# Left keys of two neighbouring head groups in one pass of 64x32 tiles

## The chip, the cores and the metric

The kernel runs on one core of one Trainium2 chip. The metric is the device time of one execution in microseconds (us), given as the median of several runs. A core has TensorE (PE in the profile, with its weight loads as PEld), VectorE (DVE), ScalarE (ACT), GpSimd (POOL) and SyncE (SP); each follows its own instruction list, and semaphores hold them together. Matmuls write into PSUM, which has eight banks, each 128 partitions by 512 float32.

## The reference

Inputs are q, k and v of 8 batches, 12 heads, 448 positions and 64 dimensions. Queries and keys are normalized by their root mean square, then comes softmax attention, and the result goes through a feed-forward network that has no nonlinearity but a product:

```
q_n, k_n = rmsnorm(q, g_q), rmsnorm(k, g_k)
scores = q_n @ k_n.T / sqrt(64)
attn = softmax(scores)            # over the 448 keys
x = (attn @ v) as [3584 tokens, 768]
out = ((x @ w1) * (x @ w2)) @ w3 @ w_out     # d_ff = 1024
```

## The kernel before

**Tiling.** The 96 heads are taken as 24 head groups `i` of HQ = 4 heads; three groups make a batch. All matmuls work on parts of the 128x128 array, several at a time: a pass is one set of matmuls that fill the array together and stream 448 (or 384) columns once. Scores come out transposed, with keys on the partitions. A head has 448 keys, that is three blocks of 128 and 64 left over. The left keys of two heads share one 128-partition tile `Pr`: partitions 0 to 63 hold those of one head and 64 to 127 those of the other.

**Scores** (`do_score`, L602): seven units a group, each of four matmuls of 64x64 tiles in one pass (L623), into two neighbouring banks, row half `u` into bank `u`. ScalarE takes the exponential of both banks in one instruction (L645) into the tile `P`, or `Pr` for the seventh unit. There are three `P` buffers; the third lies in the space of `w_outs` and is used once the product w3·w_out is made.

**Values** (`do_pv_kind`, L667): for each group three kinds: 0 is the sums of the exponentials (weights of ones), 1 and 2 are the two halves of the 64 value dimensions. A kind is J = 4 passes of four 128x32 tiles, one column tile a head, all into one bank (L677). The first three passes take the full blocks of keys, the fourth takes `Pr`. As `Pr` holds two heads, the value tile's fourth block is zero in the half that belongs to the other head (memset at L1149), and for the sums `ones[:, 1]` and `ones[:, 2]` are zero in one half. After kind 0 ScalarE makes the reciprocal as Ln and Exp (L692, L693); after kinds 1 and 2 VectorE multiplies it into `xT` (L712).

**FFN** (`Pair`, `do_pass`, L753 to L786): once three groups have filled a batch's `xT`, its FFN becomes a stock of pairs in `waiting`. A pair uses two neighbouring banks in two phases; in each phase a row half writes one of the banks, and at the hand-over (L741) they swap, after a wait through another engine's queue. At most two pairs are open. Names in the profile: `xT,w1s` and `xT,w2s` are the first layer, `w34s,abT` the second; `w34s` is w3·w_out.

**Order.** All instruction orders are written by a planner that runs when the kernel is built: it simulates the engines with fixed durations and at each moment lets `pe_try` (L1070) choose TensorE's next work. It goes on with a block of values that is begun (`pv_state`); else with a running pair; else with transposes, a score (if two neighbouring banks are idle and fewer than two scores are out), a pair that is past its hand-over, values (`pv_ready`, with two idle banks), or a new pair. `pv_ready` (L655) asks that all seven exponentials of the group are done and its values landed. It then starts a group alone if TensorE already is in that mode, if w3·w_out is not finished, or if fewer than `LOW` pairs are in stock; otherwise it also waits for the next group, so that two groups follow each other. `load_v` (L352) brings a group's values in four transfers on POOL's queue, planned when the buffer of four groups earlier is free.

Of the kernel before, what the change touches and what calls it, by code (L numbers as in the profile page):

```python
# [19 lines left out]
INF = float("inf")  # L20
SEM = 0.05
# [174 lines left out]
def kernel(  # L196
# [13 lines left out]
    nc = tc.nc  # L210
# [33 lines left out]
    MAX_PAIRS = 2  # L244
    MARGIN = 0.25
    LOW = 2
    AHEAD_W3 = 4
    EARLY = 4
    STOCK = 14
# [102 lines left out]
    def load_v(i, z):  # L352


        b, m = divmod(i, NQB)
        g, hi = divmod(z, 2)
        p0 = HP * (g ^ hi)
        j0, j1 = (J, NJ) if hi else (0, J)
        src = v[b, HQ * m : HQ * (m + 1)].rearrange("h (p j) d -> p h j d", j=NJ)
        nc.gpsimd.dma_start(  # L360
            out=v_bufs[i % 4][p0 : p0 + HP, g::2, 0 : j1 - j0].rearrange(
                "p h j d -> p h (j d)"
            ),
            in_=src[:, g::2, j0:j1].rearrange("p h j d -> p h (j d)"),
        )
# [236 lines left out]
    def do_score(t, z):  # L602
        n = next_score[0]
        next_score[0] += 1
        last_score[0] = t
        i, g = divmod(n, NU)
        s = st[i]
        if g == 0:
            x = min(range(3), key=lambda x: (p_free(x) > t, x))
            s["P"] = p_bufs[x]  # L610
            p_used[x] = i
            s["Pr"] = p_pool.tile([NP, 2, S], BF, tag="Pr", name="Pr")
        took = pass_us(S) + into("n")
        qkT, sc = s["qkT"], ps_all[:, z : z + 2]
        for c in range(2):
            if g < 2 * NF:
                pr, blk = divmod(g, NF)
                j = blk if c == pr else J + blk
            else:
                pr, j = c, NF  # L620
            cols = slice(HP * pr, HP * pr + HP)
            for u in range(2):
                nc.tensor.matmul(  # L623
                    out=sc[HP * c : HP * c + HP, u, 0:S].rearrange(
                        "p (j s) -> p j s", j=NJ
                    ),
                    lhsT=qkT[u * D : (u + 1) * D, 1, j, cols],
                    rhs=qkT[u * D : (u + 1) * D, 0, :, cols],
                    start=True, stop=True, tile_position=(u * D, HP * c),
                )  # L630
        dst = (
            s["P"][:, pr::2, blk, :] if g < 2 * NF else s["Pr"]
        )
        bank_at[z] = bank_at[z + 1] = INF
        out_scores[0] += 1

        def done(e):
            bank_at[z] = bank_at[z + 1] = e + SEM
            out_scores[0] -= 1
            p_at[i].append(e + SEM)  # L640

        at = t + took + TO_ENGINE - pass_us(S) + 0.187
        add(
            "ACT", 0.80, QUAD * i + 1.8 * g,
            lambda: nc.scalar.activation(out=dst, in_=sc[:, :, 0:S], func=AF.Exp),  # L645
            needs=[lambda: at - 0.187], done=done,
        )
        if g == NU - 1:
            qkT_used[i] = t + took + 0.2
        return took  # L650
# [1 line left out]
    next_pv = [0]  # L652
    pv_state = []

    def pv_ready(t):  # L655
        i = next_pv[0]
        if i >= NQ or all_of(p_at[i], NU) > t or landed[i]["v"] + SEM > t:
            return False
        b, m = divmod(i, NQB)
        if m == 0 and b >= 3 and x_used[b - 3] > t:  # L660
            return False
        stock = sum(p.name != "w" for p in waiting)
        if mode[0] == "v" or all_of(w34_at, CF) > t or i + 1 >= NQ or stock < LOW:
            return True
        return all_of(p_at[i + 1], NU) <= t and landed[i + 1]["v"] + SEM <= t

    def do_pv_kind(t, i, kind, z):  # L667
        s = st[i]
        b, m = divmod(i, NQB)
        ps = ps_all[:, z, 0:S]  # L670
        for j in range(J):
            for hd in range(HQ):
                if kind:
                    w = v_bufs[i % 4][:, hd, j, kind - 1 :: 2]
                else:
                    w = ones[:, 0 if j < NF else 1 + hd % 2, :]
                nc.tensor.matmul(  # L677
                    out=ps[hd * HALF : (hd + 1) * HALF, :],
                    lhsT=w,
                    rhs=s["P"][:, hd, j, :] if j < NF else s["Pr"][:, hd // 2, :],  # L680
                    start=(j == 0), stop=(j == J - 1),
                    tile_position=(0, hd * HALF),
                )
        took = J * pass_us(S) + into("v")
        at = t + took + TO_ENGINE_WIDE - pass_us(S)
        bank_at[z] = INF
        if kind == 0:
            s["r_at"] = INF

            def reciprocal():  # L690
                s["r"] = att_pool.tile([128, S], FP, tag="r", name="r")
                nc.scalar.activation(out=s["r"], in_=ps, func=AF.Ln)  # L692
                nc.scalar.activation(out=s["r"], in_=s["r"], func=AF.Exp, scale=-1.0)  # L693

            def done(e):
                bank_at[z] = e - 0.48 + SEM
                s["r_at"] = e + SEM

            add("ACT", 1.06, -1000.0, reciprocal, needs=[lambda: at], done=done)
            return took  # L700
        if b not in xT:
            xT[b] = x_pool.tile([128, CM, S], BF, tag="xT", name="xT")

        def mul_done(e):
            bank_at[z] = e + SEM
            x_at[b].append(e + SEM)
            if len(x_at[b]) == CM:
                push_ffn(b)

        add(  # L710
            "DVE", 0.53, -1000.0,
            lambda: nc.vector.tensor_tensor(  # L712
                out=xT[b][:, 2 * m + kind - 1, :], in0=ps, in1=s["r"], op=MULT
            ),
            needs=[lambda: at, lambda: s["r_at"]], done=mul_done,
        )
        if kind == 2:
            pv_end[i] = t + took + 0.2
            v_free[i % 4] = t + took + 0.2
            if i + 4 < NQ:  # L720
                plan_load_v(i + 4, -1.0)
        return took

# [339 lines left out]
    def pe_step(t):  # L1065

        took = pe_try(t, t - MARGIN)
        return pe_try(t, t) if took is None else took

    def pe_try(t, r):  # L1070
        idle = idle_banks(r)
        if pv_state:
            i, kind = pv_state[0]
            z = single(idle)
            if z is None:
                return None
            took = do_pv_kind(t, i, kind, z)
            pv_state.clear()
            if kind == 2:
                next_pv[0] += 1  # L1080
            else:
                pv_state.append((i, kind + 1))
            return took
        if mode[0] == "v" and len(idle) >= 1 and pv_ready(r):
            i = next_pv[0]
            took = do_pv_kind(t, i, 0, single(idle))
            pv_state.append((i, 1))
            return took
        two = adjacent(idle)
        score = score_ready(r) and out_scores[0] < 2 and two is not None  # L1090
        hungry = free["ACT"] <= t + 0.3 and out_scores[0] == 0
        if mode[0] == "t":
            took = any_turn(t, r, idle, 1)
            if took is not None:
                return took
        if running[0] and running[0].ready() <= r:
            if score and hungry:
                return do_score(t, two)
            return do_pass(running[0], t)
        took = any_turn(t, r, idle, 2)  # L1100
        if took is not None:
            return took
        new = next_pair(r)
        late = [p for p in pairs if p.ready() <= r]
        if score:
            left = [z for z in idle if z not in (two, two + 1)]
            if hungry or late or new is None or adjacent(left) is not None:
                return do_score(t, two)
        if late:
            return do_pass(late[0], t)  # L1110
        want_pv = pv_ready(r)
        if want_pv and len(idle) >= 2:
            i = next_pv[0]
            took = do_pv_kind(t, i, 0, single(idle))
            pv_state.append((i, 1))
            return took
        if two is not None and new is not None and not want_pv:
            waiting.remove(new)
            start_pair(new, two)
            return do_pass(new, t)  # L1120
        if next_pv[0] == NQ and not waiting and not pairs and last_x[0] < 2 and idle:
            if tile_at(B // 2 - 1, NT - 1) + SEM <= r:
                return do_last(t, single(idle))
        return any_turn(t, r, idle, 1)
# [125 lines left out]
```

## Time and profile before

| what | value |
|---|---|
| median of 7 runs | 363.49 us (361.83 to 364.42) |
| profiled execution | 363.53 us, span 361.8 us |
| granted TensorE clock | 0.997 |
| PE busy | 348.9 us (96%), 7326 matmuls |
| ACT busy | 263.0 us (73%) |
| DVE busy | 207.3 us (57%) |
| matmuls of values and sums on full blocks | 864 (480 + 240 + 96 + 48) |
| matmuls of left keys (`Pr`) | 288 (192 + 96) |
| exponentials (L645) | 168, 915 to 921 ns each |

The span is the time from the first to the last instruction on the core; the execution's own time is measured around it and is 1.7 us longer. A matmul of 448 columns is listed with about 0.35 us, but the next pass starts 0.19 us after it, since matmuls overlap in the array: passes are priced by the distance of their starts. The busy time of PE counts the overlapped time once.

### The profile page before, as it was taken

Reading aid. Unit: us, or ns where it says so; the run is one execution under the profiler, and the core shown is the slowest. Engines: PE = TensorE matmul, PEld = TensorE weight load, DVE = VectorE, ACT = ScalarE, POOL = GpSimd, SP = SyncE. Lnnn points to the kernel's source line nnn. Section 1 sums busy time; section 2 is a strip of 40 time slices with the busy share of each in tenths; the row PEclk is TensorE's granted clock in tenths of the full one; section 3 lists DMA queues with packets and bytes.
Section 4 is the critical chain, followed back from the end, with each engine's and each line's share of the span. In section 5 each row is a group of like instructions: output and inputs, shape, how many; then the busy total and the mean of one; then the engine's idle time right before and its main releaser. Section 6 shows DMA issues by size and latency. Waiting matters only on the chain.

```text
span 361.8 us, 16128 instructions
## 1 busy us (share of the span) xinstructions
PE 348.9 (96%) x7326; PEld 225.5 (62%) x7326; DVE 207.3 (57%) x293; ACT 263.0 (73%) x375; POOL 75.4 (21%) x132
## 2 busy tenths in 40 slices
PE   8699999999899999999999899999999999999994
PEld 3477676656565665568765565666666666666672
DVE  5278378897679598858768677456631320222200
ACT  5867969999999997788989798768776733222131
POOL 8267351313205013220130402200400000000000
PEclk9999999999999999999999999999999999999998
DMA  8999999679995789996499949921561005100056
GB/s 193 251 260 180 257 287 266 95 168 242 171 300 112 169 147 185 280 226 150 124 217 234 170 72 224 259 56 34 74 141 45 4 2 134 47 4 2 16 132 164
DMA packets 68360, 55.11 MB, mean 152 GB/s; under 512 B 44932, under 2 KB 62244, under 8 KB 68292
## 3 DMA queue, kind: packets, MB, share of 16 engines
q1 hardware_dynamic: 49904, 36.61, 42.7%
q0 software_dynamic: 18016, 16.92, 27.8%
q8 instruction: 57, 0.93, 1.1%
q10 hardware_dynamic: 372, 0.56, 0.4%
q14 instruction: 11, 0.09, 0.1%
HBM read 46.66 MB, written 11.01 MB: 159 GB/s over the span
## 4 chain that ended last, share of the span: by engine, by line
PE 81%; DMA 5%; ACT 5%; DVE 4%; issue 2%; POOL 1%; POOLq 0%; DVEq 0%; ACTq 0%
PE ps_all L760 59%; PE ps_all L677 12%; PE ps_all L623 7%; DMA w_outs<-in_moe_w_out_dram 4%; ACT P L645 3%; DMA qkT<-qks 2%; DVE abT L843 1%; DVE ssq L418 1%; PE ps_all L1005 1%; DVE qks L441 1%; PE ps_all L948 1%; DVE xT L712 1%; PE ps_all L1027 1%; ACT o_sb L322 0%; ACT Pr L645 0%
## 5 line engine op out<-in xcount | busy, mean ns | idle before, releaser
L645 ACT ACTIVATE P<-ps_all 128x896 bf16<-128x896 f32 x120 | 105.0, 919 | 11.0 <-PE ps_all L623 10.7
L360 POOL DMA_DIRECT2D v_sb<-in_v_dram x96 | 57.3, 610 | 175.5 <-PE ps_all L677 119.4
L760 PE MATMUL ps_all<-xT,w2s 64*64 64x448 bf16 x1536 | 90.3, 350 | 0.2 <-issue 0.2
L760 PE MATMUL ps_all<-xT,w1s 64*64 64x448 bf16 x1536 | 88.5, 350 | 1.0 <-POOLq L745 1.0
L760 PE MATMUL ps_all<-w34s,abT 64*64 64x384 bf16 x1728 | 79.8, 323 | 0.4 <-DVE abT L843 0.3
L843 DVE TENSOR_TENSOR abT<-ps_all,a_sb 128x896 bf16<-128x896 f32 x32 | 34.8, 1089 | 64.6 <-PE ps_all L760 63.0
L760 PEld LDWEIGHTS <-abT 64*64 64x64 bf16 x1728 | 52.7, 107 | 20.4 <-POOLq L745 0.8
L623 PE MATMUL ps_all<-qkT 64*64 64x448 bf16 x672 | 61.2, 352 | 3.6 <-ACT P L645 1.9
L760 PEld LDWEIGHTS <-w1s 64*64 64x64 bf16 x1536 | 47.9, 107 | 26.3 <-POOLq L745 1.4
L760 PEld LDWEIGHTS <-w2s 64*64 64x64 bf16 x1536 | 48.4, 107 | 25.4 <-issue 0.8
L418 DVE TENSOR_REDUCE ssq<-sq 128x14 f32<-128x896 f32 (+1 forms) x50 | 51.4, 1042 | 17.2 <-ACT sq L411 17.0
L441 DVE TENSOR_TENSOR qks<-qk_sb,al 128x448 bf16<-128x448 f32 x96 | 55.7, 618 | 5.4 <-ACT al L430 5.2
L411 ACT ACTIVATE sq<-qk_sb 128x896 f32<-128x896 f32 (+1 forms) x50 | 45.3, 917 | 2.8 <-DMA qk_sb<-in_q_dram 2.1
L322 ACT ACTIVATE a_sb<-ps_all 128x896 bf16<-128x896 f32 x23 | 21.1, 916 | 30.4 <-PE ps_all L760 30.2
L712 DVE TENSOR_TENSOR xT<-ps_all,r 128x448 bf16<-128x448 f32 x48 | 27.7, 618 | 14.7 <-ACT r L693 13.3
L623 PEld LDWEIGHTS <-qkT 64*64 64x64 bf16 x672 | 22.1, 106 | 18.6 <-issue 8.4
L322 ACT ACTIVATE o_sb<-ps_all 128x768 f32<-128x768 f32 (+1 forms) x19 | 14.4, 759 | 23.0 <-PE ps_all L760 21.5
L677 PEld LDWEIGHTS <-v_sb 128*32 128x32 bf16 x768 | 21.4, 97 | 15.6 <-issue 0.8
L677 PE MATMUL ps_all<-P,v_sb 128*32 128x448 bf16 x480 | 30.3, 352 | 0.1
L328 DVE COPY o_sb<-ps_all 128x768 f32<-128x768 f32 (+1 forms) x12 | 10.3, 857 | 28.0 <-ACT o_sb L322 16.2
L760 PE MATMUL ps_all<-w_outs,w3T 64*64 64x384 bf16 x512 | 24.2, 323 | 0.8 <-DMA w_outs<-in_moe_w_out_dram 0.8
L645 ACT ACTIVATE w_outs<-ps_all 128x896 bf16<-128x896 f32 x24 | 21.5, 915 | 4.3 <-PE ps_all L623 4.2
(56 smaller groups left out, 236.2 us busy)
## 6 DMA issues: line engine op xcount, KB each, us to landing
out_dram<-o_sb SPq DMA_DIRECT2D x54, 192.0 KB, 3.7
qk_sb<-in_q_dram SPq DMA_DIRECT2D x18, 448.0 KB, 5.7
qk_sb<-in_k_dram SPq DMA_DIRECT2D x18, 448.0 KB, 6.9
v_sb<-in_v_dram POOLq DMA_DIRECT2D x48, 64.0 KB, 4.8
v_sb<-in_v_dram POOLq DMA_DIRECT2D x48, 48.0 KB, 4.9
qk_sb<-in_q_dram POOLq DMA_DIRECT2D x5, 448.0 KB, 9.9
qk_sb<-in_k_dram POOLq DMA_DIRECT2D x5, 448.0 KB, 10.7
w3s<-in_moe_w_dram POOLq DMA_DIRECT2D x8, 256.0 KB, 6.0
```

The source lines that it names most:

```text
L322: nc.scalar.activation(out=out, in_=in_, func=AF.Copy, scale=1.0 if by is None else by)
L328: nc.vector.tensor_copy(out=out, in_=in_)
L360: nc.gpsimd.dma_start(out=v_bufs[i % 4][p0 : p0 + HP, g::2, 0 : j1 - j0].rearrange("p h j d -> p h (j d)"), in_=src[:, g::2, j0:j1].rearra ...
L411: nc.scalar.activation(out=s["sq", t][:, x0:x1], in_=src[:, t, x0:x1], func=AF.Square)
L418: nc.vector.tensor_reduce(out=s["ssq"][:, t, x0:x1], in_=s["sq", t][:, x0:x1], axis=AX, op=ADD)
L441: nc.vector.tensor_tensor(out=s["qks"][:, t, :, x], in0=src[:, t, x], in1=s["alpha"][:, t, x].unsqueeze(2).broadcast_to([NP, NJ, D]), op=MULT,
L623: nc.tensor.matmul(out=sc[HP * c : HP * c + HP, u, 0:S].rearrange("p (j s) -> p j s", j=NJ), lhsT=qkT[u * D : (u + 1) * D, 1, j, cols], rh ...
L645: lambda: nc.scalar.activation(out=dst, in_=sc[:, :, 0:S], func=AF.Exp),
L677: nc.tensor.matmul(out=ps[hd * HALF : (hd + 1) * HALF, :], lhsT=w, rhs=s["P"][:, hd, j, :] if j < NF else s["Pr"][:, hd // 2, :], start=(j ...
L712: lambda: nc.vector.tensor_tensor(out=xT[b][:, 2 * m + kind - 1, :], in0=ps, in1=s["r"], op=MULT),
L760: mm = nc.tensor.matmul(out=ps_all[64 * h : 64 * h + 64, p.bank + z, 0 : p.n], lhsT=lhsT[64 * r : 64 * r + 64, 64 * h : 64 * h + 64], rhs= ...
L843: nc.vector.tensor_tensor(out=abT[bp][:, f0 : f0 + 2, odd * S : (odd + 1) * S], in0=ps_all[:, z : z + 2, 0:S], in1=a_sb[b, f0], op=MULT,)
```

## The change

The values are no longer done group by group with four passes a kind. Where two neighbouring groups `i` and `i + 1` are ready, they are done as one block. The left keys of both go through one pass of eight 64x32 tiles for each kind (`do_pv_rest`): a tile takes 64 rows, one half of `Pr`, and 32 columns, one head; no zeros are multiplied. So that the eight tiles fill the array, the halves of `Pr`, of the left values and of the zeros in `ones` are turned round in every second group: head `hd` of group `i` lies in half `(hd + i) % 2`. The pass writes two banks, one for each group, and each bank gets columns from both row halves. The full blocks follow in passes of four 128x32 tiles as before (`do_pv_main`, three passes a kind and group), which accumulate into the same banks.

A joint block is started when both groups are ready and `PV_BANKS` = 4 banks are idle; then neither a score nor a new pair is started before it. As many kinds as there are pairs of idle banks, up to three, have their left pass first; the other kinds have it at the end, after their full blocks. If the second group is not ready, but all its scores have been issued, the planner waits for it; else a single group is done as before, with four passes a kind, under the former conditions (low stock, w3·w_out not finished).

```diff
@@ load_v
-        p0 = HP * (g ^ hi)
+        p0 = HP * (g ^ hi ^ i % 2)
@@ do_score
-                j = blk if c == pr else J + blk
+                j = blk if c == pr ^ i % 2 else J + blk
             else:
-                pr, j = c, NF
+                pr, j = c ^ i % 2, NF
@@ pv_ready becomes pv_one and pv_size
+    def pv_one(i, t):
         if i >= NQ or all_of(p_at[i], NU) > t or landed[i]["v"] + SEM > t:
             return False
         b, m = divmod(i, NQB)
-        if m == 0 and b >= 3 and x_used[b - 3] > t:
-            return False
+        return not (m == 0 and b >= 3 and x_used[b - 3] > t)
+
+    def pv_size(t):
+        i = next_pv[0]
+        if not pv_one(i, t):
+            return 0
+        if i + 1 >= NQ:
+            return 1
+        if pv_one(i + 1, t):
+            return 2
+        if next_score[0] >= (i + 2) * NU - SOON:
+            return 0
         stock = sum(p.name != "w" for p in waiting)
-        if mode[0] == "v" or all_of(w34_at, CF) > t or i + 1 >= NQ or stock < LOW:
-            return True
-        return all_of(p_at[i + 1], NU) <= t and landed[i + 1]["v"] + SEM <= t
+        return 1 if stock < LOW or all_of(w34_at, CF) > t else 0
@@ do_pv_kind becomes do_pv_rest and do_pv_main
+    def do_pv_rest(t, i, kind, banks, first):
+        for hd in range(HQ):
+            for x in range(2):
+                g = HP * ((hd + i + x) % 2)
+                nc.tensor.matmul(
+                    out=ps_all[hd * HALF : (hd + 1) * HALF, banks[x], 0:S],
+                    lhsT=(
+                        v_bufs[(i + x) % 4][g : g + HP, hd, NF, kind - 1 :: 2]
+                        if kind
+                        else ones[g : g + HP, 0, :]
+                    ),
+                    rhs=st[i + x]["Pr"][g : g + HP, hd // 2, :],
+                    start=first, stop=not first,
+                    tile_position=(g, hd * HALF), skip_group_check=True,
+                )
+        took = 0.2 + into("r")
...
+    def do_pv_main(t, i, kind, z, nj, first, last):
+        s = st[i]
+        for j in range(nj):
+            for hd in range(HQ):
+                nc.tensor.matmul(
+                    out=ps_all[hd * HALF : (hd + 1) * HALF, z, 0:S],
+                    lhsT=value_weights(i, hd, j, kind),
+                    rhs=s["P"][:, hd, j, :] if j < NF else s["Pr"][:, hd // 2, :],
+                    start=(first and j == 0), stop=(last and j == nj - 1),
+                    tile_position=(0, hd * HALF), skip_group_check=not (first and last),
+                )
...
@@ start_pv is new
+        firsts = range(min(3, len(idle) // 2) if size == 2 else 0)
...
+        pv_state.extend(rest(kind) for kind in firsts)
+        pv_state.extend(main(kind, x) for kind in range(3) for x in range(size))
+        if size == 2:
+            pv_state.extend(
+                lambda t, idle, kind=kind: rest(kind)(t, idle)
+                for kind in range(len(firsts), 3)
+            )
@@ pe_try
-        if mode[0] == "v" and len(idle) >= 1 and pv_ready(r):
...
+        size = pv_size(r)
+        if mode[0] == "v" and len(idle) >= 1 and size == 1:
+            return start_pv(t, 1, idle)
+        if size == 2 and len(idle) >= PV_BANKS:
+            return start_pv(t, 2, idle)
         two = adjacent(idle)
-        score = score_ready(r) and out_scores[0] < 2 and two is not None
+        score = score_ready(r) and out_scores[0] < 2 and two is not None and size != 2
...
-        if want_pv and len(idle) >= 2:
+        if size == 1 and len(idle) >= 2:
+            return start_pv(t, 1, idle)
-        if two is not None and new is not None and not want_pv:
+        if two is not None and new is not None and not size:
```

More of the change, by code (lines that the diff above doesn't have):

```diff
@@ L246 @@
     LOW = 2
+    PV_BANKS = 4
+    SOON = 0
     AHEAD_W3 = 4
@@ L653 @@
     pv_state = []
-    def pv_ready(t):
-        i = next_pv[0]
+    def pv_one(i, t):
         if i >= NQ or all_of(p_at[i], NU) > t or landed[i]["v"] + SEM > t:
@@ L659, in pv_ready @@
         b, m = divmod(i, NQB)
-        if m == 0 and b >= 3 and x_used[b - 3] > t:
-            return False
-        stock = sum(p.name != "w" for p in waiting)
-        if mode[0] == "v" or all_of(w34_at, CF) > t or i + 1 >= NQ or stock < LOW:
-            return True
-        return all_of(p_at[i + 1], NU) <= t and landed[i + 1]["v"] + SEM <= t
-    def do_pv_kind(t, i, kind, z):
+        return not (m == 0 and b >= 3 and x_used[b - 3] > t)
[9 more added lines that the diff above has]
+            return 0
+        stock = sum(p.name != "w" for p in waiting)
+        return 1 if stock < LOW or all_of(w34_at, CF) > t else 0
@@ new lines, in value_weights @@
+    def value_weights(i, hd, j, kind):
+        if kind:
+            return v_bufs[i % 4][:, hd, j, kind - 1 :: 2]
+        return ones[:, 0 if j < NF else 1 + (hd + i) % 2, :]
+    def do_pv_rest(t, i, kind, banks, first):
[14 more added lines that the diff above has]
+        took = 0.2 + into("r")
+        if not first:
+            for x in range(2):
+                pv_summed(i + x, kind, banks[x], t + took)
+        return took
@@ new lines, in do_pv_main @@
+    def do_pv_main(t, i, kind, z, nj, first, last):
[9 more added lines that the diff above has]
+                )
+        took = nj * pass_us(S) + into("v")
+        if last:
+            pv_summed(i, kind, z, t + took)
+        return took
@@ L668, in do_pv_kind, with pv_summed @@
+    def pv_summed(i, kind, z, end):
         s = st[i]
@@ L670, in do_pv_kind @@
         ps = ps_all[:, z, 0:S]
[L671 to L686, printed above, removed]
+        at = end + TO_ENGINE_WIDE - pass_us(S)
         if kind == 0:
@@ L699, in do_pv_kind @@
             add("ACT", 1.06, -1000.0, reciprocal, needs=[lambda: at], done=done)
-            return took
+            return
         if b not in xT:
@@ L717, in do_pv_kind @@
         if kind == 2:
-            pv_end[i] = t + took + 0.2
-            v_free[i % 4] = t + took + 0.2
+            pv_end[i] = v_free[i % 4] = end + 0.2
             if i + 4 < NQ:
                 plan_load_v(i + 4, -1.0)
-        return took
     pairs = []
@@ L1068, in pe_step, with start_pv, rest, main @@
         return pe_try(t, t) if took is None else took
+    def start_pv(t, size, idle):
+        i = next_pv[0]
+        next_pv[0] += size
+        banks = {}
+        firsts = range(min(3, len(idle) // 2) if size == 2 else 0)
+        for n, z in enumerate(sorted(idle)[: 2 * len(firsts)]):
+            banks[divmod(n, 2)] = z
+            bank_at[z] = INF
+        def rest(kind):
+            both = [banks[kind, x] for x in range(2)]
+            return lambda t, idle: do_pv_rest(t, i, kind, both, kind in firsts)
+        def main(kind, x):
+            def step(t, idle):
+                z = banks.get((kind, x))
+                if z is None:
+                    z = single(idle)
+                    if z is None:
+                        return None
+                    banks[kind, x] = z
+                    bank_at[z] = INF
+                one = size == 1
+                return do_pv_main(
+                    t, i + x, kind, z, J if one else NF, kind not in firsts,
+                    one or kind in firsts,
+                )
+            return step
+        pv_state.extend(rest(kind) for kind in firsts)
[4 more added lines that the diff above has]
+                for kind in range(len(firsts), 3)
+            )
+        return pv_state.pop(0)(t, idle)
     def pe_try(t, r):
@@ L1072, in pe_try @@
         if pv_state:
[L1073 to L1082, printed above, removed]
-            return took
-        if mode[0] == "v" and len(idle) >= 1 and pv_ready(r):
[L1085 to L1088, printed above, removed]
+            took = pv_state[0](t, idle)
+            if took is not None:
+                pv_state.pop(0)
+            return took
+        size = pv_size(r)
[3 more added lines that the diff above has]
+            return start_pv(t, 2, idle)
         two = adjacent(idle)
-        score = score_ready(r) and out_scores[0] < 2 and two is not None
+        score = score_ready(r) and out_scores[0] < 2 and two is not None and size != 2
         hungry = free["ACT"] <= t + 0.3 and out_scores[0] == 0
@@ L1110, in pe_try @@
             return do_pass(late[0], t)
-        want_pv = pv_ready(r)
-        if want_pv and len(idle) >= 2:
[L1113 to L1116, printed above, removed]
-        if two is not None and new is not None and not want_pv:
+        if size == 1 and len(idle) >= 2:
+            return start_pv(t, 1, idle)
+        if two is not None and new is not None and not size:
             waiting.remove(new)
```

## The prediction

> **What bounds the kernel now.** I read the page's head first, then its chain, then who TensorE waits for, then stretches, then TensorE's timeline around a block of values.
>
> ```profile
> span 361.8 us, 16128 instructions
> PE 348.9 (96%) x7326; PEld 225.5 (62%) x7326; DVE 207.3 (57%) x293; ACT 263.0 (73%) x375; POOL 75.4 (21%) x132
> ...
> PE 81%; DMA 5%; ACT 5%; DVE 4%; issue 2%; POOL 1%; POOLq 0%; DVEq 0%; ACTq 0%
> PE ps_all L760 59%; PE ps_all L677 12%; PE ps_all L623 7%; DMA w_outs<-in_moe_w_out_dram 4%; ACT P L645 3%; DMA qkT<-qks 2%; DVE abT L843 1%; DVE ssq L418 1%; PE ps_all L1005 1%; DVE qks L441 1%; PE ps_all L948 1%; DVE xT L712 1%; PE ps_all L1027 1%; ACT o_sb L322 0%; ACT Pr L645 0%
> ```
>
> TensorE is the chain: 81% of it, and 12% is L677, the passes of values and sums, which the change edits. A busy TensorE counts overlapping matmuls, so I check by stretches (us, then busy time of PE, PEld, DVE, ACT, POOL):
>
> ```profile
> 60.00:92.00 32.00, 32.00 (x682) 19.55 (x679) 28.63 (x40) 30.97 (x47) 7.72 (x13) 1.00 0.85 180
> 92.00:132.00 40.00, 38.54 (x808) 25.34 (x804) 29.68 (x41) 39.40 (x56) 7.94 (x14) 1.00 0.88 179
> 132.00:292.00 160.00, 157.92 (x3384) 101.43 (x3380) 101.12 (x139) 131.15 (x184) 27.70 (x47) 1.00 0.73 144
> 292.00:361.80 69.80, 65.08 (x1436) 42.33 (x1428) 10.60 (x12) 16.65 (x21) 0.00 (x0) 0.98 0.25 65
> ```
>
> There are two regimes. Up to about 132 us ACT is as full as TensorE (30.97 of 32, 39.40 of 40 us). From 132 us on ACT has room (131 of 160) and TensorE has not (157.9 of 160). After 292 us, when the last values are done, TensorE still has 65 us to do. A batch's FFN is 96 passes at 0.189 us (priced below) and 54 of 384 columns at 0.162 us (four lie between 264.10 and 264.75 us in the last view below), 26.9 us, so some 38 us of that is older work: attention may be late by tens of us there at no cost, and a pass saved is time saved. At 92 us it is the other way round:
>
> ```profile
> 91.39 0.36 PE L677 MATMUL ps_all<-Pr,v_sb 128*32 128x448 bf16 x4
> 91.68 0.57 PE L623 MATMUL ps_all<-qkT 64*64 64x448 bf16 x8
> 93.08 1.19 PE L623 MATMUL ps_all<-qkT 64*64 64x448 bf16 x12 [0.83 <-ACT P L645]
> 94.08 1.33 PE L760 MATMUL ps_all<-xT,w1s 64*64 64x448 bf16 x24
> ```
>
> Here TensorE has nothing but scores and waits for an exponential until batch 1's values give it FFN work at 94 us. What TensorE saves before that is waited away again, unless the attention chain itself gets shorter.
>
> **The price of a pass and of a switch.** The start times of the two-group block at 106 us:
>
> ```profile
> 105.93 0.39 PE L623 MATMUL ps_all<-qkT 64*64 64x448 bf16 x4
> 106.25 0.75 PE L677 MATMUL ps_all<-P,ones 128*32 128x448 bf16 x12
> 106.83 0.36 PE L677 MATMUL ps_all<-Pr,ones 128*32 128x448 bf16 x4
> 107.02 0.74 PE L677 MATMUL ps_all<-P,v_sb 128*32 128x448 bf16 x12
> ...
> 110.61 0.36 PE L677 MATMUL ps_all<-Pr,v_sb 128*32 128x448 bf16 x4
> 110.90 0.57 PE L623 MATMUL ps_all<-qkT 64*64 64x448 bf16 x8
> ```
>
> The first and last of the 24 passes start 4.36 us apart, so a pass takes 4.36 / 23 = 0.189 us; that of left keys (107.02 − 106.83) as much as any, though half of its rows hold zeros. From 110.61 to 110.90 is 0.29 us: a change of tile shape costs 0.10 us over a pass, at exit. At entry (105.93 to 106.25) it is 0.13, with a wait; I take 0.09 to 0.10 per switch. The block is 4.65 us from 106.25 to 110.90: 24 passes and the exit switch. The trace shows eleven such two-group blocks (starting at 44, 75, 106, 128, 147, 177, 195, 219, 252, 265 and 288 us) and two single ones (23 and 89 us).
>
> **The change, part by part.**
>
> *Passes.* Two groups need 3 kinds x 2 x 4 = 24 passes now, and 3 x 2 x 3 + 3 = 21 afterwards. The 96 matmuls of a block stay 96 (72 and 3 x 8). So −3 x 0.189 = −0.567 us a joint block. Conditions for a single (low stock, next group's scores not all issued) are as before, so I keep eleven joint blocks and two singles. Of these the two before 92 us (groups 1-2 and 3-4) count nothing: see below. Nine count: −5.10 us.
>
> *Switches.* 64x32 tiles are a third shape. With six free banks the three left passes come first and add one switch; with four, two come first and one last, two switches. The trace shows both occupancies, so 1.5 x 0.09 x 9 = +1.2 us.
>
> *The left pass itself.* Eight tiles at once were never run here. From below: 0.189, as in every pass of four tiles. From above: the two row halves one after the other, 0.378. The nearest row is the score pass (L623), 64x64 tiles on both row halves and both column halves, at 0.19 us; its four starts lie within 0.04 us. I take 0.20: 27 x 0.011 = +0.3 us. A rule of the Trainium skill speaks against this: "TensorEngine Tiling (Array Packing)", section "Gotcha 1: PSUM Pressure", says that "Different row tiles cannot access same PSUM bank simultaneously". Every pass of the kernel now obeys it (in L623 and L760 each row half has its own bank, and the hand-over at L741 exists for it). The new pass sends both halves into each of its two banks, though into different quarters of the partitions. By the row the sum is −2.25 us; by the rule 27 x 0.178 = 4.8 us more, so about +2.6 us. I take the row, since no quarter of a bank is ever written by two halves.
>
> *Entry.* The first left pass needs Pr of both groups at once, where the second group's was needed 1.9 us into the block or later; it also wants four banks free rather than two, and once both groups are ready neither a score nor a new FFN pair is started. Queued behind on TensorE is everything; ACT waits for the scores. At 106 us the last Pr exponential ended at 105.46; then the score at 105.93 would not be issued, one pair holds two banks in its hand-over, one score two more until 106.26: four are free, no wait. At 265 us:
>
> ```profile
> 263.48 0.92 ACT L645 ACTIVATE Pr<-ps_all 128x896 bf16<-128x896 f32 x1
> ...
> 264.32 1.76 ACT L645 ACTIVATE w_outs<-ps_all 128x896 bf16<-128x896 f32 x2
> 264.58 0.12 PEld L623 LDWEIGHTS <-qkT 64*64 64x64 bf16 x4
> 264.75 0.36 PE L623 MATMUL ps_all<-qkT 64*64 64x448 bf16 x4
> ```
>
> The pass before ends near 264.75, Pr is done at 264.40, and the score whose exponential runs from 264.32 holds its banks until 265.2; with two pairs open that is a wait of up to 0.5 us. A running pair, or one that comes out of its hand-over, covers it otherwise. Bounds a block: 0 and one exponential, 0.92. I take 0.15, nearer to the first: x 9 = +1.35 us. If that cover were gone, it would be 8 us.
>
> *Inside the block.* Sums of both groups come first, so the reciprocals stand back to back on ACT (0.54 + 0.58 us each, twice) and the multiplications on DVE (0.62 each, four) crowd at the end. TensorE has 12 to 15 passes, over 2.3 us, before it needs a bank again: nothing. The freed P buffers and value buffers of the first group come some 2 us later: the third P buffer, in w_outs, and loads planned four groups ahead hide that.
>
> *Before 92 us.* At 44 us group 2's last exponential ends at 45.9; the block starts about 2 us later, and w3 products fill TensorE. At 75 us TensorE starts 0.5 us before Pr of group 4 is done (75.36); now it waits for it, with no FFN pair ready, and gives back what the shorter block saves. Nothing gained or lost: 0.
>
> *The rest.* Turned halves in scores and value loads are the same instructions and the same four transfers a group. On SP and POOL nothing is added. 0.
>
> Sum: −5.10 + 1.2 + 0.3 + 1.35 = −2.25 us. The profiled execution took 363.53 us around its span of 361.8, and the median is 363.49, so the sum carries over: **361.3 us**, span about 359.6.
>
> **Rivals.**
>
> *Gain kept nearly whole.* Six banks mostly free, no entry waits, early blocks gain too: 11 x (0.567 − 0.09) = 5.2 us, 358.3. For it: TensorE's own waits are few now. Against it: two or three shapes of work hold banks at every block start seen.
>
> *Waits take the place of the passes.* 0.3 to 0.5 us at each entry, or ACT starved: each block withholds one or two scores, 0.81 us of exponential each, which matters only before 132 us (three blocks, 2.5 us). That gives 362.5 to 365, mostly no change. For it: ACT at 39.40 of 40 us. Against it: blocks are half a us shorter, and squares and reciprocals fill ACT meanwhile.
>
> *Slower: the row halves serialize in a bank.* Place: the 33 left passes. Price: 33 x 0.178 = 5.9 us over my sum, so 367.1. It decides from 2.25 / 33 = 0.07 us a pass over my 0.20, a left pass of 0.27. For it: the rule above, and no pass of that kind in the trace. Against it: separate quarters of the partitions.
>
> **How the numbers follow.** A difference under 0.3%, 1.1 us, can't be told from none. The likeliest case, 359.8 to 362.4, gets 0.50; the whole gain 0.12; waits 0.26, of which 0.18 end within 0.3% and 0.08 slower; serialized halves 0.12. So faster 0.62, same 0.18, slower 0.20. The range 358.6 to 365.4 leaves out the serialized case and the ends of the others; the faster cases alone span 358.3 to 362.4.
>
> **What would show it.** A left-pass row of 64x32 tiles, 24 matmuls a joint block, 264 in all, with starts 0.19 to 0.21 us apart: at 0.38 the slower rival holds. Joint blocks of 4.2 to 4.3 us from first pass to the next work, in place of 4.65. TensorE waiting for Pr (L645) at the blocks at most 0.2 us on average, and batch 1's first FFN pass at about 94 us as now: if that moves to 96, attention is starved. Fewer joint blocks than ten would break the sum as well.

## The result

The changed kernel takes 360.05 us in the median of 15 runs (358.28 to 365.62), the kernel before 363.37 us over 36 runs. The ratio is 0.9908, with a 95% interval of 0.9888 to 0.9928: 3.3 us faster (2.6 to 4.1). The forecast was 361.3 us: the right direction, with a gain that was too small by a third. The first profiled execution was a disturbed one (span 363.7 us at a granted clock of 0.991), so the profile shown here is that of the same kernel run again, `a_again` below.

The head of its page and its chain:

```profile
span 359.2 us, 16097 instructions
PE 346.4 (96%) x7326; PEld 220.0 (61%) x7326; DVE 208.1 (58%) x293; ACT 261.7 (73%) x375; POOL 75.4 (21%) x132
...
PE 73%; ACT 17%; DMA 5%; DVE 2%; issue 2%; SPq 0%; POOLq 0%; ACTq 0%; DVEq 0%
PE ps_all L799 50%; PE ps_all L711 9%; ACT P L648 8%; PE ps_all L626 6%; DMA qk_sb<-in_q_dram 3%; ACT sq L414 3%; PE ps_all L1221 2%; PE ps_all L690 2%; DMA qkT<-qks 2%; ACT Pr L648 2%; ACT w_outs L648 1%; DVE xT L753 1%; PE ps_all L1066 1%; PE ps_all L1044 1%; PE ps_all L987 1%
```

The number of matmuls is the same, 7326, and PE's busy time is 2.5 us less. TensorE's idle time, the span less the busy time, is 12.8 us; it was 12.9. Values and sums held 12% of the chain (L677); now L711 and L690 hold 9% and 2%. ACT's share of the chain grew from 5% to 17%.

The left passes stand under one line. This view lists them with duration (least, median, most), first and last start, and shape:

```profile
L690 PE MATMUL ps_all<-Pr,v_sb x176: 346/349/362, 47.2 to 291.3; 64*32 64x448 bf16 x176
L690 PE MATMUL ps_all<-Pr,ones x88: 359/359/361, 47.0 to 287.2; 64*32 64x448 bf16 x88
```

That is 264 matmuls: eleven joint blocks of 24, as forecast. TensorE's timeline of the block that answers to the one at 106 us before:

```profile
108.74 0.76 PE L799 MATMUL ps_all<-xT,w1s 64*64 64x448 bf16 x12
109.44 0.38 PE L690 MATMUL ps_all<-Pr,ones 64*32 64x448 bf16 x8
109.63 0.37 PE L690 MATMUL ps_all<-Pr,v_sb 64*32 64x448 bf16 x8
109.94 1.32 PE L711 MATMUL ps_all<-P,ones 128*32 128x448 bf16 x24
111.08 2.44 PE L711 MATMUL ps_all<-P,v_sb 128*32 128x448 bf16 x48
113.46 0.38 PE L690 MATMUL ps_all<-Pr,v_sb 64*32 64x448 bf16 x8
113.77 0.57 PE L799 MATMUL ps_all<-xT,w2s 64*64 64x448 bf16 x8
```

Two left passes come first (109.44 and 109.63; 0.20 us apart by the exact starts), one last (113.46): the form for four banks. From 109.63 to 109.94 is 0.30 us by the exact starts, a pass of 0.19 and 0.11 for the change of tile shape; the change back before 113.46 costs 0.10 and the exit 0.12. From first pass to next work it is 4.33 us, where it was 4.65: 0.32 us less. Nine of the eleven blocks have that length. The first (at 47 us) has six banks, one switch fewer, and 4.21 us; one (at 249 us) has a wait of 0.25 us in it. Added over all thirteen blocks, exact starts give 52.6 us, against 56.6 us before; 0.6 us of the difference were waits inside two of the old blocks.

Two stretches of the forecast, in the same columns:

```profile
92.00:132.00 40.00, 38.63 (x840) 25.53 (x836) 34.81 (x48) 36.00 (x54) 7.15 (x12) 1.00 1.03 201
132.00:292.00 160.00, 158.32 (x3444) 99.95 (x3436) 97.85 (x135) 136.08 (x190) 28.49 (x48) 1.00 0.72 141
```

After 132 us TensorE is as full as it was. ACT did less between 92 and 132 us (36.00 in place of 39.40 us). Holding back scores ahead of a block accounts for about 1.4 us of that, as a run below without it shows. ACT made it up afterwards (136 in place of 131 us), where it has room.

### The profile page after: what moved, and what is told of

It is laid out like the page before. It is cut to its first block, busy times and chain, and to the rows that moved or that the text cites. A ratio compares the mean times of both kernels' runs of the same rounds, so it can differ in the third digit from the quotient of the medians.

```text
span 363.7 us, 16097 instructions
## 1 busy us (share of the span) xinstructions
PE 348.1 (96%) x7326; PEld 220.2 (61%) x7326; DVE 207.9 (57%) x293; ACT 261.5 (72%) x375; POOL 75.4 (21%) x132
## 4 chain that ended last, share of the span: by engine, by line
PE 74%; ACT 13%; DMA 8%; DVE 2%; issue 2%; POOL 1%; SPq 0%; POOLq 0%; ACTq 0%
PE ps_all L799 54%; PE ps_all L711 10%; PE ps_all L626 7%; ACT P L648 5%; DMA w_outs<-in_moe_w_out_dram 4%; DMA qkT<-qks 2%; ACT sq L414 2%; PE ps_all L690 2%; ACT Pr L648 1%; DMA qk_sb<-in_q_dram 1%; DVE xT L753 1%; PE ps_all L987 1%; PE ps_all L1044 1%; ACT w_outs L648 1%; ACT r L734 1%
## 5 line engine op out<-in xcount | busy, mean ns | idle before, releaser
L799 PE MATMUL ps_all<-xT,w1s 64*64 64x448 bf16 x1536 | 90.2, 352 | 0.1
L626 PE MATMUL ps_all<-qkT 64*64 64x448 bf16 x672 | 61.0, 353 | 5.3 <-DMA qkT<-qks 2.7
L799 PEld LDWEIGHTS <-w2s 64*64 64x64 bf16 x1536 | 47.3, 108 | 26.1 <-issue 2.2
L799 PEld LDWEIGHTS <-w1s 64*64 64x64 bf16 x1536 | 46.9, 108 | 25.9 <-issue 1.1
L324 ACT ACTIVATE o_sb<-ps_all 128x768 f32<-128x768 f32 (+1 forms) x22 | 17.0, 771 | 27.8 <-PE ps_all L799 26.2
L324 ACT ACTIVATE a_sb<-ps_all 128x896 bf16<-128x896 f32 x20 | 18.3, 917 | 23.0 <-PE ps_all L799 23.0
L626 PEld LDWEIGHTS <-qkT 64*64 64x64 bf16 x672 | 21.5, 107 | 18.9 <-issue 5.7
L799 PE MATMUL ps_all<-w_outs,w3T 64*64 64x384 bf16 x512 | 25.6, 338 | 2.9 <-DMA w_outs<-in_moe_w_out_dram 2.7
L711 PE MATMUL ps_all<-P,v_sb 128*32 128x448 bf16 x480 | 26.0, 353 | 0.0
L711 PEld LDWEIGHTS <-v_sb 128*32 128x32 bf16 x592 | 15.9, 97 | 12.1
L648 ACT ACTIVATE Pr<-ps_all 128x896 bf16<-128x896 f32 x24 | 22.0, 918 | 0.1
```

What stands on the lines that cost most here:

```text
L324: nc.scalar.activation(out=out, in_=in_, func=AF.Copy, scale=1.0 if by is None else by)
L626: nc.tensor.matmul(out=sc[HP * c : HP * c + HP, u, 0:S].rearrange("p (j s) -> p j s", j=NJ), lhsT=qkT[u * D : (u + 1) * D, 1, j, cols], rh ...
L711: nc.tensor.matmul(out=ps_all[hd * HALF : (hd + 1) * HALF, z, 0:S], lhsT=value_weights(i, hd, j, kind), rhs=s["P"][:, hd, j, :] if j < NF ...
L799: mm = nc.tensor.matmul(out=ps_all[64 * h : 64 * h + 64, p.bank + z, 0 : p.n], lhsT=lhsT[64 * r : 64 * r + 64, 64 * h : 64 * h + 64], rhs= ...
```

## The experiments

All times are medians of runs taken beside runs of the kernel before; the ratio is to those. The changed kernel stands at 360.05 and 360.44 us in its two measurements, which I take together as 360.2.

**The changed kernel again.**

> The changed kernel once more, for an undisturbed profile. By the theory that the saved passes are the gain: about 360 us, ratio to before 0.991; eleven joint blocks, ten of them 4.33 us from first pass to next work in place of 4.65, left passes 0.19 to 0.20 us apart, no new wait of TensorE for Pr at the blocks except the one at about 75 us; batch 1's first FFN pass at 94 to 95 us, as before. By the rival that the new order of work (scores held back, four banks) is the gain: TensorE's idle time between passes falls by 2 us or more.

360.44 us, ratio 0.9912 (0.9877 to 0.9946). Eleven joint blocks, nine of 4.33 us. The rival's sign, 2 us less idle time of TensorE, is absent (12.8 us after 12.9). One wait that the forecast expected did not come. At 75 us the block was to wait for Pr of group 4; on ACT's timeline that exponential now ends at 74.35, and TensorE's timeline has the block at 74.78:

```profile
73.44 0.91 ACT L648 ACTIVATE Pr<-ps_all 128x896 bf16<-128x896 f32 x1
```

```profile
73.71 1.14 PE L799 MATMUL ps_all<-xT,w2s 64*64 64x448 bf16 x20
74.78 0.38 PE L690 MATMUL ps_all<-Pr,ones 64*32 64x448 bf16 x8
```

In the new order the exponential comes a us earlier (75.36 before) and the block as early as it was (74.89); nothing is waited for there. Batch 1's first FFN pass starts at 93.80 us (94.08 before), but at 90.82 to 93.80 TensorE has second-layer work where it had none before. A wait comes later instead, for the transfer into `qkT`:

```profile
90.82 1.47 PE L799 MATMUL ps_all<-w34s,abT 64*64 64x384 bf16 x32
...
93.80 0.93 PE L799 MATMUL ps_all<-xT,w1s 64*64 64x448 bf16 x16
...
99.34 0.38 PE L626 MATMUL ps_all<-qkT 64*64 64x448 bf16 x4 [0.83 <-DMA qkT<-qks]
```

So TensorE's busy time between 92 and 132 us hardly changed: 38.63 us, 38.54 before. Ahead of 92 us it now idles, which it did not before. The rows are the kernel before, the changed kernel, and the next run, which has the new order without the joint pass:

```profile
24.00:92.00 68.00, 68.00 (x1452) 44.65 (x1445) 54.68 (x79) 60.24 (x92) 26.07 (x44) 1.00 0.98 215
24.00:92.00 68.00, 66.92 (x1420) 42.79 (x1416) 53.66 (x76) 58.95 (x89) 26.26 (x44) 1.00 0.96 211
24.00:92.00 68.00, 66.69 (x1396) 43.93 (x1392) 55.07 (x79) 58.20 (x89) 26.39 (x44) 1.00 0.95 203
```

That is 1.08 us of idle time in the changed kernel. The run without the joint pass saves nothing in its early blocks and idles 1.31 us there, so the idle time seems to come with the new order and not with the saving. These are single traces: `e2` below, in the changed kernel's order, idles 0.62 us, and part of the 1.08 and 1.31 us is a stall near 46 us that the last section takes up.

**Without the joint pass.** The order of a joint block stays; the left keys go back into four passes a kind.

```diff
-        firsts = range(min(3, len(idle) // 2) if size == 2 else 0)
+        joint = size == 2 and False
+        firsts = range(min(3, len(idle) // 2) if joint else 0)
...
-                one = size == 1
+                one = not joint
...
-        if size == 2:
+        if joint:
```

> Two ready groups still start together, with four idle banks and scores held back, but every kind has its own four passes with half-empty left keys: 24 passes again, no 64x32 tiles. By the theory that the passes are the gain: the whole gain goes, 363.4 us (362.7 to 364.5), ratio to before 0.998 to 1.003. By the rival that the new order is the gain: 360 to 361 us, ratio 0.991 to 0.994.

362.65 us, ratio 0.9975 (0.9955 to 0.9995). A block is 4.65 us long again (112.50 to 117.16), with the left keys again in passes of their own:

```profile
112.50 0.75 PE L711 MATMUL ps_all<-P,ones 128*32 128x448 bf16 x12
113.08 0.36 PE L711 MATMUL ps_all<-Pr,ones 128*32 128x448 bf16 x4
...
116.86 0.36 PE L711 MATMUL ps_all<-Pr,v_sb 128*32 128x448 bf16 x4
117.16 0.38 PE L799 MATMUL ps_all<-xT,w1s 64*64 64x448 bf16 x4
```

Some three quarters of the gain go with the passes: 2.2 us beside the changed kernel's 360.44, 2.5 us beside the 360.2. The rest, 0.25% under the kernel before, was expected by neither theory; the interval only just leaves out no difference. It would be the new order of work, but that is not shown. The planner made ten joint blocks and four singles here, in place of eleven and two, so the split is not exact.

**A bank for each row half.** The rule of the Trainium skill that the forecast weighed ("TensorEngine Tiling (Array Packing)", "Gotcha 1: PSUM Pressure"), tried directly:

```diff
-                    out=ps_all[hd * HALF : (hd + 1) * HALF, banks[x], 0:S],
+                    out=ps_all[hd * HALF : (hd + 1) * HALF, banks[g // HP], 0:S],
```

> In the left pass each row half writes a bank of its own, as the skill's rule on banks asks, in place of both halves in each bank. The left keys of half of the heads thereby end in the neighbouring group's sums, so the output is another; the work is the same. By the theory that halves may share a bank if they write different quarters of the partitions: no difference to the changed kernel, 360 us (359.3 to 360.9), left passes 0.19 to 0.20 us apart in both. By the rival that sharing a bank costs something: the left pass is shorter than in the changed kernel and the time lies 1 us or more under it.

359.36 us, ratio 0.9897 (0.9852 to 0.9942), which can't be told from the changed kernel's 0.9912. The timeline of the same block:

```profile
108.66 0.38 PE L690 MATMUL ps_all<-Pr,ones 64*32 64x448 bf16 x8
108.86 0.37 PE L690 MATMUL ps_all<-Pr,v_sb 64*32 64x448 bf16 x8
...
112.99 0.76 PE L799 MATMUL ps_all<-xT,w2s 64*64 64x448 bf16 x12
```

Again 4.33 us from 108.66 to 112.99; by exact starts all eleven blocks are as long as the changed kernel's to within 3 ns, the one with the 0.25 us wait too. So two row halves in one bank cost nothing here, where they write different quarters of the partitions. What they cost in one quarter was not tried.

**Six banks.**

```diff
-    PV_BANKS = 4
+    PV_BANKS = 6
```

> A joint block waits for six idle banks, so that all three left passes come first and a block has one more change of tile shape in place of two. By the theory that entries are covered by running pairs: 11 x 0.12 us less, about 359 us, blocks of 4.21 us. By the rival that the two further banks are waited for: each entry costs 0.3 us or more and the time is 361 to 363 us.

358.88 us, ratio 0.9867 (0.9827 to 0.9906). All three left passes come first now:

```profile
110.62 0.38 PE L690 MATMUL ps_all<-Pr,ones 64*32 64x448 bf16 x8
110.83 0.56 PE L690 MATMUL ps_all<-Pr,v_sb 64*32 64x448 bf16 x16
...
114.83 0.38 PE L799 MATMUL ps_all<-xT,w1s 64*64 64x448 bf16 x4
```

The block is 4.21 us (110.62 to 114.83) in ten of eleven blocks; the first had that length already, so nine are 0.12 us shorter. Two of these blocks and a single one begin 0.09 to 0.14 us later than a bare switch would have them, and the eleventh block has a wait of 0.35 us inside. Those are the waits that show at the blocks.

> Six idle banks before a joint block, once more. By the theory that a change of tile shape saved in ten blocks is 10 x 0.12 us: 1.2 us under the changed kernel, ratio to before 0.987 to 0.990. By the rival that the first result was a favourable chip: ratio 0.991 as the changed kernel's.

The same kernel again gave 359.89 us, ratio 0.9915 (0.9885 to 0.9945). The first result was indeed a good one. By the ratios the two together lie some 0.7 us under the changed kernel's two; the summed lengths of the blocks are 1.15 and 0.77 us less in the two traces. That it beats the changed kernel isn't shown by these intervals. It does beat the kernel before in both.

**Scores not held back**, with four banks and then with six.

```diff
-        score = score_ready(r) and out_scores[0] < 2 and two is not None and size != 2
+        score = score_ready(r) and out_scores[0] < 2 and two is not None
```

> As the changed kernel, but scores are not held back once two groups are ready. By the theory that TensorE's passes alone set the time and attention has slack: no difference to the changed kernel (360.2 us; 359.4 to 361). By the rival that holding scores back starves ACT before 132 us: 1 us or more faster, and ACT's idle time between 92 and 132 us falls from 4 us to under 2. By a third, that a block then starts later because scores hold its banks: 361 us or more.

359.68 us, ratio 0.9912 (0.9889 to 0.9934): no difference. ACT is busy 37.4 of the 40 us between 92 and 132, 1.4 us more than in the changed kernel, and the end doesn't move:

```profile
92.00:132.00 40.00, 38.59 (x840) 26.10 (x832) 35.82 (x49) 37.38 (x56) 7.14 (x12) 1.00 1.04 209
```

So holding back scores starves nothing that matters; with four banks it isn't needed either. Two blocks enter 0.1 and 0.2 us late.

> Six idle banks before a joint block and scores not held back. By the theory that entries are covered: as with six banks alone, 358.9 us (358 to 359.8). By the rival that scores that go on take the banks: blocks start later, TensorE waits at entries, 360 us or more.

371.52 us, ratio 1.0231 (1.0205 to 1.0257): 11 us slower than the changed kernel. Who TensorE waits for (total, times, longest):

```profile
PE ps_all L690 <- ACT P L648: 2.1, 4, 1.0
PE ps_all L626 <- ACT P L648: 2.0, 6, 0.4
PE ps_all L626 <- DVE o_sb L330: 1.7, 2, 0.9
PE ps_all L690 <- ACT w_outs L648: 1.4, 3, 0.5
```

Left passes (L690) now wait for exponentials that still hold a bank, and scores (L626) for evacuations. In the stretch 132 to 292 us TensorE does 3222 matmuls, where it did 3444:

```profile
132.00:292.00 160.00, 151.38 (x3222) 97.67 (x3224) 99.07 (x137) 129.49 (x182) 28.52 (x48) 0.99 0.72 145
```

This is the forecast's rival, waits in place of passes. By exact starts the blocks begin 3.9 us late in all, the worst by 1.1 us, and are 4.2 us longer in all than with six banks undisturbed. Of these, 1.7 us fall in the block that begins at 202.6 us: passes there are 0.35 us apart, while the granted clock was 0.5 for 3.4 us. The likely course, argued and not tested: every score that goes on takes two of the six banks, a new pair is not started either, and TensorE runs dry. Either piece alone is harmless: four banks with scores going on, or six banks with scores held back.

**Time added to early and to late blocks.** The forecast counted two early blocks at nothing. To test that, TensorE's time was added instead, first as 20 more left passes (`HQ_LIST` holds the four heads; the late run has group 18 in place of group 1; the planner is told of the longer pass):

```diff
+        more = 20 if (i, kind) == (1, 0) else 0
-        for hd in range(HQ):
+        for hd in HQ_LIST * (1 + more):
```

> The same 20 more passes in the joint block of groups 18-19 (at about 249 us). By both theories they reach the end whole: 360.2 + 3.9 = 364.1 us (363.3 to 365).

364.15 us, ratio 1.002 (1.000 to 1.004), as expected: 20 passes of 0.19 us or 3.8 us added, 4 us later. The 168 left matmuls stand in one row, 21 passes at 0.19 us:

```profile
248.88 4.17 PE L692 MATMUL ps_all<-Pr,ones 64*32 64x448 bf16 x168
252.86 0.37 PE L692 MATMUL ps_all<-Pr,v_sb 64*32 64x448 bf16 x8
```

> The first left pass of the joint block of groups 1-2 (at about 47 us) is made 21 times in place of once: 20 more passes of 0.19 to 0.2 us, some 3.9 us of TensorE's time in an early block, with the same output. By the theory that TensorE has time to spare before batch 1's FFN begins at 94 us: less than 2.5 us of it reach the end, 361 to 362.7 us. By the rival that a pass costs the same everywhere: 364.1 us.

367.72 us, ratio 1.0135 (1.0109 to 1.0161): 7.5 us later. But the block itself had grown by 8.2 us, not by 3.9:

```profile
46.93 2.65 PE L692 MATMUL ps_all<-Pr,ones 64*32 64x448 bf16 x104
51.40 1.71 PE L692 MATMUL ps_all<-Pr,ones 64*32 64x448 bf16 x64 [1.82 <-issue]
...
57.92 1.49 PE L713 MATMUL ps_all<-P,v_sb 128*32 128x448 bf16 x25 [2.06 <-issue]
```

Twice TensorE stood still for about 2 us and waited for nothing that the profile shows ("issue"). So the run mixes two causes, and it was made again with few instructions, as 18 idle matmuls over the whole array ahead of the first left pass (`e9` in the block of groups 1-2, as shown; `e10` with 3 in place of 1, in that of groups 3-4):

```diff
+        more = 18 if (i, kind) == (1, 0) else 0
+        for _ in range(more):
+            nc.tensor.matmul(
+                out=ps_all[:, banks[0], :], lhsT=warm_t[:, 0:128], rhs=warm_t,
+                start=True, stop=True,
+            )
```

> 18 idle matmuls of 128x128 tiles and 512 columns (0.216 us each, 3.9 us) ahead of the first left pass of groups 1-2 at about 47 us; they write the bank that this pass then starts afresh. Few instructions, so that a lack of instructions can't add to it. By the theory that an early block's time reaches the end like any other's: 360.2 + 3.9 = 364.1 us (363.3 to 365). By the step of the prediction that TensorE waits this time away before 94 us: under 362.7 us.

> The same 18 matmuls ahead of the block of groups 3-4 at about 75 us, where TensorE's backlog is lowest. By the theory that early time counts: 364.1 us (363.3 to 365), more if the scores that it holds up starve ACT for longer than it lasts. By the step of the prediction: under 362.7 us.

364.98 us, ratio 1.0056 (1.0029 to 1.0082), and 365.75 us, ratio 1.0055 (1.0022 to 1.0089). In `e9` the added work is where it was meant to be, without a stall:

```profile
47.73 4.06 PE L689 MATMUL ps_all<-warm_t 128*128 128x512 bf16 x17
...
95.19 0.38 PE L626 MATMUL ps_all<-qkT 64*64 64x448 bf16 x4 [0.42 <-ACT P L648]
```

By the medians they end 4.8 and 5.5 us after the changed kernel, by the ratios 5.3 us each: the 3.9 us come through whole, with 0.9 to 1.6 us on top. TensorE's idle time did not shrink to take them up: between 24 and 92 us it is 0.99 us in `e9` and 1.83 in `e10`, after 1.08 in the changed kernel. In `e9` three scores from 95 us on wait 0.4 us each for exponentials, so attention had become late. The planner also makes another order after such an edit (in `e9` groups 5 and 6 became a joint block), so the excess itself isn't explained. That early time counts in full is shown for time added; for time saved it is inferred, and 3.9 us is far more than the 0.76 us that the two early blocks save.

## Why the prediction was right, and where it was not

*What bounds the kernel, and the passes.* Right. 24 passes became 21, and taking the joint pass away takes most of the gain away.

*The left pass.* Taken as 0.20 us, measured 0.20 after a change of shape and 0.19 in a row of them. (The sum counted 27 left passes and the slower rival 33; there are 33.) The rule on banks did not bind: the slower rival that rested on it is refuted by these 0.20 us in the changed kernel, where the rule would have made them 0.38, and a bank for each half changed nothing.

*Switches.* Taken as 1.5 a block at 0.09 us. Ten of eleven blocks took the four-bank form with two more switches, and those between 64x32 and 128x32 cost 0.10 to 0.11 us. A block saves 0.32 us, where the sum had about 0.40 before entries: over nine blocks the sum's costs were 0.7 us too small.

*Entry.* This term was mis-sized: 0.15 us a block, 1.35 us in all; measured nothing. In the kernel before the last matmul ahead of each of the thirteen blocks starts 0.25 to 0.28 us before it, and in the changed kernel likewise. The occupancy I counted at the old block starts was that of an order in which scores went on up to the block; in the new one they stop, and FFN passes stand directly before the joint blocks. The stop of scores can't be the whole reason: with scores going on only two blocks entered late, by 0.3 us together. The warning attached to the term (8 us if the cover is gone) is borne out in part: with six banks and scores going on the blocks began 3.9 us late, within a loss of 11 us.

*Early blocks.* "Nothing gained or lost: 0" is not settled. Its wait at 75 us didn't appear, and its ground, that TensorE's time before 92 us is waited away, failed for time added: that reached the end in full. A likely reason is that a block of values lies on attention's own way, with the next group's scores behind it on TensorE. For the 0.76 us saved there the runs don't decide. The total can't: without the early blocks the measured terms give 9 x 0.32 = 2.9 us, with them 10 x 0.32 + 0.44 = 3.6 us, and the measured 2.6 to 4.1 us hold both. The idle time ahead of 92 us grew by about as much as was saved, but it grew without the joint pass too.

So the number was near in part by errors that offset each other: entries too dear by 1.35 us, switches too cheap by 0.7 us, and perhaps 0.76 us of early blocks left out. The run without the joint pass puts the passes at 2.2 to 2.5 us and leaves some 0.8 us to the new order, a term that the forecast did not have; the spread of the runs is too wide to set this against the 2.9 or 3.6 us.

## What to carry to other kernels

A half-empty pass costs as much as a full one, so two of them packed into one pass pay even after two more changes of tile shape; count those changes per block, for they took nearly half of what the passes gave (0.25 of 0.57 us a block). Occupancy of banks at a block's start must be judged under the new order of work, not read off the old trace. A stretch where an engine sometimes idles is not a place where its time is free: time added there came through whole. Ask first whether the work stands ahead of the very work that is late.

## What was not expected of the hardware

Eight 64x32 tiles ran at the pace of four 64x64 ones, 0.19 us for 448 columns (21 passes from 248.88 to 252.86 us in the late run), with both row halves writing different partition quarters of the same bank.

The stalls in `e5` were new in their size: 1.82 and 2.06 us in a stretch where the DMA engines were full. A short one of the kind is in the changed kernel too:

```profile
45.59 1.47 PE L799 MATMUL ps_all<-w_outs,w3T 64*64 64x384 bf16 x24 [0.36 <-issue]
```

The DMA view of `e5` from 48 to 60 us:

```profile
DMA  9999999995799999989989999998999999999986
...
q8 instruction: 2, 0.03, 1.0%
```

The exact records have TensorE stop at 49.2 and 55.5 us, just when 16 KB instruction loads on that queue began (49.08 and 55.55 us, about 1 us each), and resume 1.4 us after each had ended. Between the two stalls TensorE ran 127 matmuls, 127 weight loads and two waits: 256 instructions. Over the whole run it has some 15000 of them and the queue 58 such loads, 259 a load; so it stopped after about one load's worth. The late run, with the same passes but quieter DMA (0.28 of the engines' time from 248 to 257 us), had two such loads inside its block (250.8 and 254.3 us) and no stall. All this fits a lack of instructions, which passes of sixteen instructions in 0.19 us use up twice as fast as those of eight; no run separated that from other causes.
